# The mask of the single slots, made on ScalarE from the cubic's factor in place of GpSimd

## The chip, the cores and the metric

The kernel runs on one core of a Trainium2 chip. The metric is the device time of one execution in microseconds (us), the median of several runs. The engines are TensorE (PE; its weight loads are PEld), VectorE (DVE), ScalarE (ACT), GpSimd (POOL) and SyncE (SP), which issues most DMAs. Each engine works its own queue in order.

## The reference

A Nystrom attention (batch 4, 8 heads, 576 positions, head dimension 64, 32 landmarks) feeds two MLPs one behind the other, with 2304 tokens, model width 512 and hidden width 2048.

```python
x = attention(q, k, v)                    # A @ Z @ C @ v per head, Z by six Newton steps
h = x @ w_in;  x = (h - tanh(h)) @ w_out  # first MLP
h = x @ w_in2
out = (h * tanh(log(1 + exp(h)))) @ w_out2
```

The change lies in the first MLP, in h - tanh(h). The kernel computes it in two ways and picks one for each element. Where |h| is under 0.28, a cubic form: h times h squared times a factor q, with q = (FB * exp(FK * h^2) + FC)^2. Elsewhere the plain difference h - tanh(h). A mask of one byte per element (0, or not 0) says where the difference is to replace the cubic.

## The kernel before

**Slots.** The first MLP is cut into 128 slots s: batch b = s // 32, half of the positions hf = s // 16 % 2, and one of 16 blocks f = s % 16 of 128 hidden units. A slot works on a tile of 128 hidden units x 288 tokens. Slots 0 to 23 and 104 to 127 are wide: they go in pairs, and an instruction has 576 columns (`vec`). Slots 24 to 103 are single, with 288 columns (`vec_one`). In the trace the single slots run from 112 to 361 us.

**One single slot.** `h1(s)` makes h on TensorE, into one of two PSUM banks of the pool ps_h (L845 to L851; from slot 32 on six matmuls with split operands). `vec_one(s)` then issues, by line of the kernel before:

- ScalarE: e = h squared (L927), t = tanh h (L928), q = exp (L931), q = Square with a bias (L932).
- GpSimd: the mask mk = (e >= FT) (L929), with FT = 0.28^2.
- VectorE: for the slot before, g = q * g (L872, in `small`) and the pick, t over g where the mask is not 0 (L876, in `pick`); for this slot g = h * e (L940) and t = h - t (L942). L942 is the last reader of the bank of h, which `h1(s + 2)` needs.

Two slots later `low_one` splits g into a high and a low part, gg: a copy on ScalarE (L123) and a subtract on GpSimd (L124). Four slots later (LAG) `y1` multiplies gg by the second weight on TensorE, 12 matmuls of 288 columns (L957, L958, L961), into the banks of y. After 16 slots ScalarE empties these banks (L973).

**Beside the slots.** The attention of the next batch and half runs in small steps between the slots, fed in by `bg`: on GpSimd a subtract (L743) and a product (L758) of the softmax, the exp between them on ScalarE (L746), transposes on VectorE (L738, L768), then the split into AT (L123, L124); and the products P of Z and the first weight, which TensorE makes in a bank of ps_m (L431), ScalarE copies (L808) and VectorE splits (L810).

**What sets the order.** For slots 0 to 103 a scheduler orders each engine's instructions by priority; `tc.high_priority(40)` lifts some of them ahead. From slot 104 on the order is as written. In the wide slots the mask is already made by ScalarE, from q (`MASK_BY_ACT` is 0, so in all of them). The constants of that form:

```python
FQ = (FB * exp(FK * FT) + FC) ** 2
FS = 1024.0
V.memset(bias_q, FS * FQ)
A.activation(out=mk, in_=q, func=ACTF.Relu, scale=-FS, bias=bias_q[:, 0:1])
```

q falls as e rises, and FQ is its value at e = FT; so FS * (FQ - q) is above 0 just where e is above FT.

Of the kernel before, what the change touches and what calls it, by code (L numbers as in the profile page):

```python
# [16 lines left out]
ACTF = mybir.ActivationFunctionType  # L17
ALU = mybir.AluOpType
# [5 lines left out]
FT = 0.28 ** 2  # L24
# [5 lines left out]
FS = 1024.0  # L30
# [3 lines left out]
def kernel(  # L34
# [73 lines left out]
    A = nc.scalar  # L108
    G = nc.gpsimd
# [19 lines left out]
    bias_q = const.tile([128, 1], F32)  # L129
# [728 lines left out]
    def low_half(s):  # L858
        gg = gg_tile(s, F32R)
        with tc.high_priority(20):  # L860
            split(sv[s], gg[:, 0], gg[:, 1], late())
        sv[s], sv[s + 1] = gg[:, :, 0], gg[:, :, 1]

    def low_one(s):
        gg = (ggs[s - 1] if s % 2 else gg_tile(s, F32R))[:, :, s % 2]
        with tc.high_priority(20):
            split(sv[s][0], gg[:, 0], gg[:, 1], late())
        sv[s] = gg

    def small(g, q):  # L870
        with tc.high_priority(40):
            V.tensor_tensor(out=g, in0=q, in1=g, op=ALU.mult)  # L872

    def pick(g, mk, t):
        with tc.high_priority(40):
            V.copy_predicated(out=g, mask=mk, data=t)  # L876
# [42 lines left out]
    def vec_one(s):  # L919
        i = s % 2  # L920
        if s == WIDE[0]:
            low_half(s - 2)
        elif s > WIDE[0] + 1:
            low_one(s - 2)
        h, e, q, mk = hp.pop(s), ES[:, i], QS[:, i], MK[-1][:, i]
        t, g = TA[:, i], (TB, TC)[s // 2 % 2][:, i]
        A.activation(out=e, in_=h, func=ACTF.Square)  # L927
        A.activation(out=t, in_=h, func=ACTF.Tanh)  # L928
        G.tensor_scalar(out=mk, in0=e, scalar1=FT, scalar2=None, op0=ALU.is_ge)  # L929
        with tc.high_priority(40):  # L930
            A.activation(out=q, in_=e, func=ACTF.Exp, scale=FK)  # L931
            A.activation(out=q, in_=q, func=ACTF.Square, scale=FB, bias=bias_c[:, 0:1])  # L932
        sv[s] = (g, t, q, mk)
        if s > WIDE[0]:
            g0, t0, q0, mk0 = sv[s - 1]
            small(g0, q0)
            yield 0
            pick(g0, mk0, t0)
            yield 0
        V.tensor_tensor(out=g, in0=h, in1=e, op=ALU.mult)  # L940
        yield 0
        V.tensor_tensor(out=t, in0=h, in1=t, op=ALU.subtract)  # L942
        yield 1
# [424 lines left out]
    def pair(s, bg):  # L1368
        cur[0] = s
        v = vec(s) if wide(s) else None  # L1370
        if s == WIDE[1]:
            two_banks()
        if v:
            h1(s)
            h1(s + 1)
        for i in (s, s + 1):
            cur[0] = i
            if not v:
                h1(i)
            if i >= LAG:  # L1380
                y1(i - LAG, 0)
            mix, tail = bg(i)
            for g in mix + tail:
                part(g)
            if i >= LAG:
                y1(i - LAG, 1)
            parts([v or vec_one(i)] + mix)
            parts(tail)
# [277 lines left out]
```

## Time and profile before

| | us |
|---|---|
| median of 3 runs | 805.53 (805.09 to 805.65) |
| profiled execution | 802.95 |
| its span, first to last instruction | 801.2 |
| PE busy | 776.9 (97%) |
| PEld busy | 694.2 (87%) |
| DVE busy | 639.0 (80%) |
| ACT busy | 576.7 (72%) |
| POOL busy | 202.7 (25%) |

The granted clock of TensorE was 1.00 of full speed over the span. Busy shares are averages over stages with different limits; matmuls are pipelined and their ends are modelled, so a busy PE is not a PE at its peak. In a row of the trace, "[1.27 <-DVE ta L942]" says that the engine had been idle for 1.27 us before the instruction, and that the end of DVE's L942 on tile ta ended that.

### The profile page before, as it was taken

The numbers are of one execution on the slowest core, as the hardware profiler recorded it, in microseconds if no ns is written. First come the engines' busy times: TensorE is split into PE (matmuls) and PEld (weight loads), VectorE is DVE, ScalarE is ACT, GpSimd is POOL, SyncE is SP. The second block draws the span as 40 slices with busy tenths as digits, with TensorE's granted clock in tenths as the row PEclk, the third lists the DMA queues.
The fourth block names the chain that finished last, engine by engine and source line by source line (L and its number), as shares of the span: only waits on it lengthen the run. The fifth ranks groups of instructions, "written<-read, shape, count | busy, mean of one in ns | idle before, by whom it ended". The sixth has DMA issues, their size and how long they took to land.

```text
span 801.2 us, 16889 instructions
## 1 busy us (share of the span) xinstructions
PE 776.9 (97%) x6246; PEld 694.2 (87%) x6247; DVE 639.0 (80%) x1391; ACT 576.7 (72%) x1351; POOL 202.7 (25%) x229
## 2 busy tenths in 40 slices
PE   8889999999999999989999999999999999999997
PEld 4656787899978999778998999998999999999997
DVE  8899899988789976987779988877566876687556
ACT  5788887787678876778999777776556655665553
POOL 0000028765678656772230000001000010001000
PEclk9999999999999999999999999999999999999999
DMA  9788822414035000331215998999998899889881
GB/s 327 299 311 301 333 90 102 148 52 138 13 112 184 6 31 1 106 110 52 83 55 207 388 324 287 357 298 346 367 327 288 283 371 312 288 286 335 293 298 53
DMA packets 79873, 171.47 MB, mean 214 GB/s; under 512 B 8752, under 2 KB 51760, under 8 KB 75696
## 3 DMA queue, kind: packets, MB, share of 16 engines
q1 hardware_dynamic: 78672, 166.73, 60.0%
q0 software_dynamic: 1120, 3.67, 1.2%
q8 instruction: 49, 0.80, 0.4%
q14 instruction: 32, 0.26, 0.1%
HBM read 133.41 MB, written 36.96 MB: 213 GB/s over the span
## 4 chain that ended last, share of the span: by engine, by line
PE 68%; DVE 13%; ACT 10%; issue 4%; POOL 2%; DMA 1%; SPq 0%; DVEq 0%; ACTq 0%; POOLq 0%
PE h L1095 25%; PE y L1095 8%; PE m L1095 4%; PE y L957 3%; PE y L958 2%; PE y L961 2%; PE hw L845 2%; PE y L952 2%; PE y L1228 2%; PE y L1230 2%; PE y L1229 2%; DVE tc L872 2%; DVE tb L872 1%; DVE tb L876 1%; ACT gg L123 1%
## 5 line engine op out<-in xcount | busy, mean ns | idle before, releaser
L1095 PE MATMUL h<-yk,P 128*128 128x256 f32 (+1 forms) x1152 | 182.7, 297 | 0.4 <-DVE yk L1005 0.2
L1095 PEld LDWEIGHTS h<-yk,P 128*128 128x128 f32 x1152 | 161.9, 188 | 6.1 <-DVE u L1170 0.5
L957 PE MATMUL y<-gg,w 128*128 128x288 f32 x448 | 132.8, 311 | 2.9 <-ACT raw L973 2.8
L958 PE MATMUL y<-gg,w 128*128 128x288 f32 x448 | 125.5, 295 | 0.0
L929 POOL TENSOR_SCALAR mk<-es 128x288 uint8<-128x288 f32 x80 | 78.6, 983 | 135.0 <-DVE tc L876 111.5
L957 PEld LDWEIGHTS y<-gg,w 128*128 128x128 f32 x448 | 84.1, 188 | 21.9 <-issue 15.3
L961 PE MATMUL y<-gg,w 128*128 128x288 f32 x448 | 95.5, 294 | 0.0
L958 PEld LDWEIGHTS y<-gg,w 128*128 128x128 f32 x448 | 84.3, 188 | 0.5
L1095 PE MATMUL y<-w,gg 128*128 128x256 f32 x516 | 73.3, 282 | 0.0
L961 PEld LDWEIGHTS y<-gg,w 128*128 128x128 f32 x448 | 71.7, 188 | 0.0
L1095 PEld LDWEIGHTS y<-w,gg 128*128 128x128 f32 x516 | 66.3, 189 | 0.3
L1170 DVE TENSOR_TENSOR w<-w,h 128x256 f32<-128x256 f32 x48 | 20.2, 421 | 56.4 <-PE h L1095 30.9
L124 POOL TENSOR_TENSOR gg<-tc,gg 128x288 fp32r<-128x288 f32 (+1 forms) x45 | 40.0, 898 | 39.7 <-ACT gg L123 35.4
L124 POOL TENSOR_TENSOR gg<-tb,gg 128x288 fp32r<-128x288 f32 (+1 forms) x44 | 40.6, 927 | 32.8 <-ACT gg L123 31.8
L162 ACT ACTIVATE top<-raw 128x512 f16<-128x512 bf16 x56 | 41.9, 783 | 7.8 <-DVE w L167 3.1
L849 PE MATMUL h<-AT,P 128*128 128x288 f32 x144 | 43.0, 299 | 3.0 <-DVE ta L942 3.0
L927 ACT ACTIVATE es<-h 128x288 f32<-128x288 f32 x80 | 32.1, 402 | 17.8 <-PE h L851 15.2
L932 ACT ACTIVATE qs<-qs,bias_c 128x288 f32<-128x288 f32 x80 | 42.7, 534 | 1.2
L1312 POOL DMA_DIRECT2D out_dram<-y x4 | 2.9, 724 | 160.3 <-DVE y L1320 160.3
L850 PE MATMUL h<-AT,P 128*128 128x288 f32 x144 | 42.5, 295 | 0.0
L851 PE MATMUL h<-AT,P 128*128 128x288 f32 x144 | 42.5, 295 | 0.0
L1150 DVE TENSOR_TENSOR gg<-x,gg 128x256 fp32r<-128x256 f32 (+1 forms) x71 | 33.1, 466 | 7.4 <-ACT x L1137 4.5
(265 smaller groups left out, 1995.2 us busy)
## 6 DMA issues: line engine op xcount, KB each, us to landing
P<-w2s SPq DMA_DIRECT2D x24, 1024.0 KB, 5.6
w<-w2t SPq DMA_DIRECT2D x92, 256.0 KB, 8.2
P<-w2s SPq DMA_DIRECT2D x24, 768.0 KB, 7.3
w<-w1s SPq DMA_DIRECT2D x24, 512.0 KB, 4.6
w2s<-P SPq DMA_DIRECT2D x8, 1024.0 KB, 5.8
raw<-in_w2i_dram SPq DMA_DIRECT2D x16, 511.8 KB, 5.0
raw<-in_w2o_dram SPq DMA_DIRECT2D x16, 511.8 KB, 4.3
raw<-in_w1o_dram SPq DMA_DIRECT2D x13, 511.8 KB, 6.2
```

Source lines behind the costliest of these rows:

```text
L124: eng.tensor_tensor(out=L, in0=src, in1=f32(H), op=ALU.subtract)
L162: A.activation(out=top[:, :, 1], in_=raw.bitcast(BF16)[:, :, 2], func=ACTF.Copy)
L849: mm(p, P[:, g, 0, c], AT[:, g, 0, :], start=(g == 0), stop=False)
L850: mm(p, P[:, g, 0, c], AT[:, g, 1, :], start=False, stop=False)
L851: mm(p, P[:, g, 1, c], AT[:, g, 0, :], start=False, stop=(g == NG - 1))
L929: G.tensor_scalar(out=mk, in0=e, scalar1=FT, scalar2=None, op0=ALU.is_ge)
L932: A.activation(out=q, in_=q, func=ACTF.Square, scale=FB, bias=bias_c[:, 0:1])
L957: mm(yps[d], w[:, 0, c], gg[:, 0, :], start=(f == 0), stop=False)
L958: mm(yps[d], w[:, 1, c], gg[:, 0, :], start=False, stop=False)
L961: mm(yps[d], w[:, 0, c], gg[:, 1, :], start=False, stop=(f == NF - 1))
L1095: mm(*args, **kw, skip_group_check=True)
L1150: V.tensor_tensor(out=gg[:, 1, :], in0=x, in1=f32(gg[:, 0, :]), op=ALU.subtract)
```

## The change

In the single slots the mask is made by ScalarE with a Relu on q, behind the Square, and no longer by GpSimd from e. The Relu is written outside the lifted priority. The diff is whole:

```diff
         t, g = TA[:, i], (TB, TC)[s // 2 % 2][:, i]
         A.activation(out=e, in_=h, func=ACTF.Square)
         A.activation(out=t, in_=h, func=ACTF.Tanh)
-        G.tensor_scalar(out=mk, in0=e, scalar1=FT, scalar2=None, op0=ALU.is_ge)
         with tc.high_priority(40):
             A.activation(out=q, in_=e, func=ACTF.Exp, scale=FK)
             A.activation(out=q, in_=q, func=ACTF.Square, scale=FB, bias=bias_c[:, 0:1])
+        A.activation(out=mk, in_=q, func=ACTF.Relu, scale=-FS, bias=bias_q[:, 0:1])
         sv[s] = (g, t, q, mk)
```

Lines 929 to 932 shift by it: exp is L931 before and L930 after, the Square L932 before and L931 after, the new Relu is L932 after. ScalarE has 80 instructions more and GpSimd 80 fewer; the orders of TensorE and of SyncE are the same row for row. VectorE has the same instructions in a slightly different order.

GpSimd in slots 57 to 61, with two subtracts and two products of the softmax (L743, L758). Before:

```order
L743 TENSOR_TENSOR c<-c,xm 128x288
L124 TENSOR_TENSOR gg<-tb,gg 128x288
L929 TENSOR_SCALAR mk<-es 128x288
L743 TENSOR_TENSOR c<-c,xm 128x288
L929 TENSOR_SCALAR mk<-es 128x288
L124 TENSOR_TENSOR gg<-tc,gg 128x288
L758 TENSOR_TENSOR c<-c,xm 128x288
L929 TENSOR_SCALAR mk<-es 128x288
L758 TENSOR_TENSOR c<-c,xm 128x288
L124 TENSOR_TENSOR gg<-tc,gg 128x288
```

And with the change:

```order
L743 TENSOR_TENSOR c<-c,xm 128x288
L124 TENSOR_TENSOR gg<-tb,gg 128x288
L743 TENSOR_TENSOR c<-c,xm 128x288
L758 TENSOR_TENSOR c<-c,xm 128x288
L124 TENSOR_TENSOR gg<-tc,gg 128x288
L758 TENSOR_TENSOR c<-c,xm 128x288
L124 TENSOR_TENSOR gg<-tc,gg 128x288
```

The three masks are gone, and the first L758 stands ahead of a gg subtract that it stood behind.

ScalarE in slot 99, where the last four banks of y of a half are emptied (L973). Before:

```order
L927 ACTIVATE es<-h 128x288
L928 ACTIVATE ta<-h 128x288
L931 ACTIVATE qs<-es 128x288
L973 ACTIVATE raw<-y 128x288
L932 ACTIVATE qs<-qs,bias_c 128x288
L973 ACTIVATE raw<-y 128x288
L808 ACTIVATE P<-m 128x512
L123 ACTIVATE AT<-c 128x288
L808 ACTIVATE P<-m 128x512
L973 ACTIVATE raw<-y 128x288 x2
L123 ACTIVATE gg<-tc 128x288 x2
```

And with the change:

```order
L927 ACTIVATE es<-h 128x288
L928 ACTIVATE ta<-h 128x288
L930 ACTIVATE qs<-es 128x288
L973 ACTIVATE raw<-y 128x288
L931 ACTIVATE qs<-qs,bias_c 128x288
L973 ACTIVATE raw<-y 128x288
L932 ACTIVATE mk<-qs,bias_q 128x288
L808 ACTIVATE P<-m 128x512 x2
L973 ACTIVATE raw<-y 128x288 x2
L123 ACTIVATE gg<-tc 128x288
```

The Relu stands ahead of L808, and the copy into AT, which stood between the two L808, has moved into the next slot.

## Rows read from the trace of the kernel before

**Rows 1.** Busy time by stretch: length; PE, PEld, DVE, ACT, POOL; clock; DMA.

```profile
112.00:139.00 27.00, 25.94 (x205) 20.51 (x203) 24.65 (x53) 20.90 (x53) 20.05 (x22) 1.00 0.17 59
139.00:172.00 33.00, 31.48 (x262) 27.29 (x262) 31.02 (x66) 26.88 (x76) 25.73 (x30) 1.00 0.39 135
172.00:214.00 42.00, 41.95 (x470) 37.98 (x470) 34.10 (x87) 31.95 (x92) 24.92 (x28) 1.00 0.22 72
214.00:240.00 26.00, 24.11 (x209) 20.09 (x209) 22.18 (x51) 18.67 (x50) 18.97 (x22) 1.00 0.25 84
240.00:270.00 30.00, 29.30 (x239) 25.44 (x237) 28.31 (x60) 25.43 (x70) 23.95 (x27) 1.00 0.36 129
270.00:311.00 41.00, 41.00 (x465) 37.63 (x466) 31.30 (x83) 30.89 (x88) 23.82 (x28) 1.00 0.05 16
311.00:339.00 28.00, 26.07 (x225) 22.05 (x224) 24.06 (x56) 19.88 (x53) 20.20 (x24) 1.00 0.22 76
339.00:361.00 22.00, 19.32 (x156) 16.64 (x155) 17.92 (x40) 16.05 (x44) 17.07 (x19) 1.00 0.33 100
```

**Rows 2.** Timeline of PE: start us, us; first h matmul of two neighbouring slots.

```profile
239.22 0.30 PE L849 MATMUL h<-AT,P 128*128 128x288 f32 x1
...
241.61 0.29 PE L849 MATMUL h<-AT,P 128*128 128x288 f32 x1
```

**Rows 3.** Waits, 112 to 360 us: us in total, times, longest us.

```profile
ACT c L746 <- POOL c L743: 7.9, 9, 1.7
...
PEld m L431 <- DVE P L810: 4.5, 6, 1.4
PEld h L849 <- DVE ta L942: 3.9, 4, 1.5
PEld y L957 <- ACT raw L973: 3.7, 4, 2.0
```

**Rows 4.** Groups by line and form, 112 to 360 us: busy us, mean ns | idle before.

```profile
L929 POOL TENSOR_SCALAR mk<-es 128x288 uint8<-128x288 f32 x80 | 78.6, 983 | 135.0 <-DVE tc L876 111.5 <-ACT es L927 18.5
...
L932 ACT ACTIVATE qs<-qs,bias_c 128x288 f32<-128x288 f32 x80 | 42.7, 534 | 1.2
...
L876 DVE COPY_PREDICATED tb<-mk,ta 128x288 f32<-128x288 uint8 x40 | 24.5, 612 | 2.6 <-POOL mk L929 0.5
...
L872 DVE TENSOR_TENSOR tc<-qs,tc 128x288 f32<-128x288 f32 x40 | 23.7, 592 | 1.7 <-ACT qs L932 1.7
...
L940 DVE TENSOR_TENSOR tb<-h,es 128x288 f32<-128x288 f32 x40 | 17.8, 445 | 11.1 <-ACT ta L928 11.1
```

**Rows 5.** Timeline of POOL, ACT and PE, 219 to 231 us, slots 58 to 61.

```profile
219.42 0.93 POOL L929 TENSOR_SCALAR mk<-es 128x288 uint8<-128x288 f32 x1
...
220.43 0.67 POOL L743 TENSOR_TENSOR c<-c,xm 128x288 f32<-128x288 f32 x1
...
221.14 0.45 ACT L746 ACTIVATE c<-c 128x288 f32<-128x288 f32 x1 [1.66 <-POOL c L743]
...
225.23 0.93 POOL L929 TENSOR_SCALAR mk<-es 128x288 uint8<-128x288 f32 x1
...
226.24 0.67 POOL L758 TENSOR_TENSOR c<-c,xm 128x288 f32<-128x288 f32 x1
...
230.97 0.40 PE L849 MATMUL h<-AT,P 128*128 128x288 f32 x1 [1.27 <-DVE ta L942]
```

**Rows 6.** Timeline of POOL and PE, 345 to 349 us, slot 99.

```profile
345.11 1.02 POOL L929 TENSOR_SCALAR mk<-es 128x288 uint8<-128x288 f32 x1
...
346.21 0.67 POOL L758 TENSOR_TENSOR c<-c,xm 128x288 f32<-128x288 f32 x1
...
348.72 0.40 PE L957 MATMUL y<-gg,w 128*128 128x288 f32 x1 [1.77 <-ACT raw L973]
```

**Rows 7.** Timeline of ACT: the Square and the start of its neighbour.

```profile
244.82 0.54 ACT L932 ACTIVATE qs<-qs,bias_c 128x288 f32<-128x288 f32 x1
245.26 0.24 ACT L507 ACTIVATE qb<-red 128x64 f32<-128x64 f32 x1
```

## Prediction, made before the changed kernel was run

> **What bounds the kernel now.** I read three views of the single slots 24 to 103 (112 to 361 us): busy time by stretch, then who waits for whom, then the order of time around the longest waits of TensorE. In the table by stretch the reader should look along the columns [rows 1]. TensorE is busy for 41.95 of 42 us and 41.00 of 41 us in the stretches 172 to 214 and 270 to 311: there it sets the pace, and ScalarE is busy for only 31.95 and 30.89. In the other six stretches TensorE falls short by 0.7 to 2.7 us, and VectorE is the fullest of the others: 31.02 of 33 us and 28.31 of 30 us (94% each) in 139 to 172 and 240 to 270, against 26.88 and 25.43 on ScalarE and 25.73 and 23.95 on GpSimd. Undisturbed, TensorE needs 2.39 us for a slot: its first h matmul starts at 239.22 and that of the next slot at 241.61 [rows 2].
>
> So at most the time that TensorE waits can be won. The waits view names three kinds: its weight loads wait 4.5 us in six places for VectorE's L810 to free a bank of ps_m, 3.9 us in four for VectorE's L942 to free a bank of ps_h, and 3.7 us in four for ScalarE's L973 to empty a bank of y; together 12.1 us. ScalarE in turn waits 7.9 us in nine places for GpSimd's L743 [rows 3].
>
> **What the change removes.** 80 masks at L929 leave GpSimd, 983 ns each, 78.6 us in all [rows 4]. Two things come of it.
>
> First, steps of the attention no longer stand behind a mask. At 219.42 GpSimd makes a mask; only at 220.43 does it start the attention's L743, and ScalarE, whose L746 stands in its queue ahead of the next slot, has been idle for 1.66 us when that is done. At 225.23 the next mask does the same to L758. At 230.97 TensorE has waited 1.27 us for L942, which has come late by both [rows 5]. A mask holds its place on GpSimd for 220.43 - 219.42 = 1.01 us. The new order has no mask between the two L743 and none between the two L758; two masks of 1.01 us cover the 1.27 us, so I take the whole wait as gone. The pattern comes again 97.2 us later, with a wait of like size: 2 x 1.3 = -2.6 us. The same happens in front of the last eviction: a mask at 345.11, L758 behind it at 346.21, and TensorE, at 348.72, has waited 1.77 us for ScalarE's L973 [rows 6]. There the new ScalarE queue also no longer has the AT copy, which waits for that L758, ahead of the last two L973. It has a mask there instead. I take the wait as gone: -1.8 us. In the first stretch two more waits of the kind of rows 3, on L942 and L810, sit behind the same pattern; the stretch falls short by 27.00 - 25.94 = 1.1 us by TensorE's busy time [rows 1], and I count that: -1.1 us. Sum: -2.6 - 1.8 - 1.1 = -5.5 us.
>
> Second, VectorE runs freer. L940, which has one operand in PSUM, takes 445 ns; L872 and L876, which have only SBUF operands of the same size, take 592 and 612 on average [rows 4]. That is 40 x (0.147 + 0.167) = 12.6 us on these two groups; their twins on the other buffer (40 each) bring it to at most twice that, 25 us. In these stretches GpSimd is busy for 174.7 us (its column added up), of which the masks are 78.6, or 45% [rows 1, 4]: I expect 0.45 x 12.6 to 0.45 x 25, 6 to 11 us of VectorE time, to come back. It lies beside TensorE's work and counts only through the waits already taken, so its price is zero; without it the six stretches would not have the room that the next step needs.
>
> The Trainium skill (SBUF — State Buffer, Who interferes with whom) says more: of a VectorE instruction with two SBUF inputs and a GpSimd instruction that reads SBUF, the second to be issued is blocked until the first has finished. By that rule a VectorE instruction behind a mask would lose up to the mask's whole length, where the averages of rows 4 show 0.15 us each; the sum by the rule is the larger gain below.
>
> **What the change adds.** 80 Relus on ScalarE. No row shows them in these slots. The nearest is the Square at L932, with the same 288 columns and also a bias from a tile: 534 ns long [rows 4], but 0.44 us from its start at 244.82 to the next start at 245.26, since neighbours overlap [rows 7]. The bounds are 0.44 and 0.53 us; I take 0.44, because the Relu stands directly behind other work in the new order: 80 x 0.44 = 35.2 us (42.7 at most). The stretches of rows 1 hold 8, 12, 13, 8, 11, 13, 9 and 6 slots, counted by the starts of the Square at L927. In the two stretches that TensorE fills, 13 Relus make 5.7 us against idle time of 10.0 and 10.1 us: hidden. In 214 to 240, 311 to 339 and 339 to 361 they make 3.5, 4.0 and 2.6 us against 7.3, 8.1 and 6.0: hidden, by time that ScalarE now spends waiting for GpSimd. In 139 to 172, 12 Relus make 5.3 us against 6.1; in 240 to 270, 11 make 4.8 against 4.6 [rows 1]. ScalarE would be 97% and over 100% full there, where no engine but TensorE is now above 94%. Packed to that 94%, the work of ScalarE needs 32.2 / 0.94 = 34.2 us and 30.2 / 0.94 = 32.1 us: 1.2 + 2.1 = 3.3 us too long. Of that I charge half, +1.6 us, since ScalarE may fall behind TensorE by two slots (two banks of h, 4.8 us) before TensorE stops, and the stretch that follows has the room to catch up. The ends are 0 and +3.3.
>
> The pick now waits for the Relu instead of GpSimd. The Relu is issued 0.44 us behind the Square and ends about as late as the multiply L872 (0.45 to 0.59 us) that starts on VectorE when the Square ends, and that stands ahead of the pick anyway: zero, up to 0.1 us a slot, and hidden where TensorE leads. Behind the pick on VectorE stands the next slot's L940. Behind the Relu stand, in places, L808 and L973, each 0.44 us later; that is in the 1.6. TensorE's and SyncE's orders are the same to the row, and the wide slots and all that follows are untouched: what is won or lost by 361 us is carried to the end, as the stages behind start from the slots and not from a clock.
>
> **Sum.** -5.5 + 1.6 = -3.9 us. The profiled execution took 802.95 us (span 801.2), 2.6 below the median of the runs, 805.53; its own changed time would be 799.0. I forecast the median: 805.5 - 3.9 = **801.6 us**. About 0.2%, 1.6 us, is what a measurement of this kernel can tell from no change.
>
> **Rivals.**
> - *ScalarE becomes the bound.* If only half of ScalarE's idle time in the six stretches can be filled (half of 6.1 + 6.1 + 7.3 + 4.6 + 8.1 + 6.0 = 38.1 us, so 19.1) while the Relus there need 23.7 us, ScalarE ends 4.6 us later, and L942, L808 and L973 come later with it, so that no wait of TensorE is won: 810.1 us. It decides once less than 62% of that idle time can be filled. For it speaks that much of the idle time lies ahead of instructions that wait in the queue's order; against it, that those waits are for GpSimd and VectorE, which become freer. The Trainium skill (ScalarE: Activation LUTs, Rules for kernel authors) is on this side: it gives relu to VectorE, not to ScalarE. The rows speak against that here, with VectorE at 94% and ScalarE at 81% and 85% where it is tightest.
> - *Nothing is won.* The waits on L810 and L973 stay, since the Relu is now ahead of L808 and L973 on ScalarE as the mask was ahead of L743 and L758 on GpSimd; what is won on L942 pays for the full stretches: 805.5, within 1.6 us.
> - *A larger gain.* All three kinds of waits go, -12.1 us, and nothing is given back: 793.4 us. It needs VectorE to win far more than rows 4 show. The rule of the blocked second instruction (the Trainium skill, SBUF — State Buffer, Who interferes with whom) would bring it about.
>
> That the Relus are not made where the text says is excluded: the order shows 80 on ScalarE and none left on GpSimd.
>
> **How the numbers follow.** The forecast's case (a gain of 1.6 to 8 us) gets 0.50: the places are clear in the trace and come twice, but the gain hangs on a ScalarE that is nearly full. The larger gain gets 0.06, no change 0.21, the slower one 0.23. Faster is 0.56, same 0.21, slower 0.23. The forecast's own range is 797.5 to 803.9; with no change and most of the slower case the range is 797.0 to 809.0, and leaves about 0.15 outside.
>
> **What would show it.** Right: by stretch, ScalarE at 95% or more in 139 to 172 and 240 to 270 and GpSimd about 79 us lower; L872 and L876 near 500 ns; no wait of TensorE on L942 near 231 and 328, none on L973 near 348; the single slots 3 to 5 us shorter, the rest as long as before. Wrong: waits of TensorE for L973, L942 or L810 that are longer than in rows 3, with ScalarE without idle time ahead of them.

## The result and the profile after

The changed kernel takes 798.29 us (median of 4 runs, 797.87 to 799.20), the kernel before 805.31 in the runs beside it (804.38 to 805.65): ratio 0.9914, 95% interval 0.9902 to 0.9926, a gain of 7.0 us where 3.9 were forecast. The profiled execution took 797.99 us, with a span of 796.2, and a granted clock of 1.00 throughout.

Where the time went is first read from the starts of ScalarE's first activation of a slot. From slot 24 to the first wide slot, 104, these rows of the timeline, before:

```profile
112.23 0.41 ACT L927 ACTIVATE es<-h 128x288 f32<-128x288 f32 x1 [1.14 <-PE h L845]
...
360.92 0.65 ACT L889 ACTIVATE es<-hw 128x576 f32<-128x576 f32 x1 [2.22 <-PE hw L851]
```

And after:

```profile
113.07 0.41 ACT L927 ACTIVATE es<-h 128x288 f32<-128x288 f32 x1 [1.14 <-PE h L845]
...
355.64 0.65 ACT L889 ACTIVATE es<-hw 128x576 f32<-128x576 f32 x1 [1.06 <-PE hw L851]
```

The single slots are 248.69 us long before and 242.57 after: 6.1 us shorter. What lies ahead of them and behind them differs by +0.8 and +0.3 us, with the same instructions in it. Counted in the same way from slot 24 on, the changed kernel has won 0.2 us by slot 57, 2.2 by slot 65, 2.4 by slot 89, 4.4 by slot 97 and 6.1 by slot 104. So the gain lies in three places: 2.0 us in slots 57 to 64, 2.0 in 89 to 96, 1.7 in 97 to 103. A second profile of the changed kernel, taken with the last experiments, has 2.0, 2.0 and 1.7 at the same places, but lies 1.4 us behind the first by slot 57: there TensorE waits 1.14 and 0.21 us for VectorE's L686 in slots 51 and 52, which it does not in the first. A reading of a single place can be trusted further than the total of one profile.

Busy time by stretch (columns as in [rows 1]; the borders follow the slots, which now come earlier):

```profile
112.00:139.00 27.00, 26.12 (x219) 20.72 (x212) 23.88 (x54) 22.44 (x58) 11.09 (x13) 1.00 0.15 48
139.00:172.00 33.00, 31.80 (x267) 27.67 (x266) 29.97 (x65) 31.36 (x87) 14.13 (x18) 1.00 0.42 144
172.00:212.00 40.00, 39.37 (x451) 35.62 (x450) 32.65 (x85) 36.51 (x103) 10.09 (x13) 1.00 0.23 76
212.00:237.00 25.00, 24.82 (x218) 20.73 (x216) 20.84 (x49) 23.07 (x61) 11.66 (x16) 1.00 0.23 82
237.00:267.00 30.00, 29.98 (x253) 26.95 (x246) 27.68 (x61) 28.43 (x80) 13.04 (x17) 1.00 0.39 133
267.00:308.00 41.00, 40.37 (x459) 36.30 (x457) 30.51 (x84) 37.34 (x104) 10.89 (x14) 1.00 0.04 16
308.00:334.00 26.00, 25.82 (x225) 22.03 (x224) 22.81 (x54) 23.33 (x61) 11.12 (x15) 1.00 0.23 82
```

ScalarE, the fourth busy time, is at 95% in 139 to 172 and in 237 to 267, as forecast, and in the latter TensorE is full: 29.98 of 30 us. But 172 to 212 and 267 to 308, in which TensorE was full before, now fall short by 0.6 us each. Right behind each of the two full stretches TensorE has a new wait of 0.58 us for VectorE's L537, at 172.74 and at 267.71:

```profile
172.74 1.49 PE L431 MATMUL m<-k,qb 64*32 64x304 f32 x16 [0.58 <-DVE mx L537]
```

Against that, two pairs of short waits around the first evictions are gone: 0.44 us on L973 and 0.22 on L942 at 152.55 and 156.25 before, 0.44 and 0.21 at 249.76 and 253.46. The two sides are about equal, so the gain of the slots does not show them. In 212 to 237 and 308 to 334 TensorE falls short by 0.2 us, where it fell short by 1.9 in the like stretches before [rows 1].

The timeline shows what happened at the first of the three places. GpSimd, the counterpart of [rows 5]:

```profile
218.67 0.67 POOL L743 TENSOR_TENSOR c<-c,xm 128x288 f32<-128x288 f32 x1
...
220.06 0.68 POOL L743 TENSOR_TENSOR c<-c,xm 128x288 f32<-128x288 f32 x1
222.40 0.67 POOL L758 TENSOR_TENSOR c<-c,xm 128x288 f32<-128x288 f32 x1 [1.66 <-DVE xm L756]
...
225.02 0.67 POOL L758 TENSOR_TENSOR c<-c,xm 128x288 f32<-128x288 f32 x1 [0.59 <-DVE xm L756]
```

No mask stands between these rows, and GpSimd waits for its own input, VectorE's xm. ScalarE's L746 comes at 219.37 without a wait and at 220.77 with one of 0.53 us, in place of 1.66. TensorE's timeline before, behind the wait of 1.27 us at 230.97 [rows 5], showed these at the first two places:

```profile
237.08 1.31 PE L431 MATMUL m<-q,kb 64*32 64x288 f32 x16 [0.61 <-DVE P L810]
...
328.18 0.40 PE L849 MATMUL h<-AT,P 128*128 128x288 f32 x1 [1.26 <-DVE ta L942]
334.29 1.31 PE L431 MATMUL m<-q,kb 64*32 64x288 f32 x16 [0.67 <-DVE P L810]
```

After, two waits are left there:

```profile
235.80 1.31 PE L431 MATMUL m<-q,kb 64*32 64x288 f32 x16 [0.18 <-DVE P L810]
...
330.79 1.31 PE L431 MATMUL m<-q,kb 64*32 64x288 f32 x16 [0.17 <-DVE P L810]
```

The wait on L942 is gone at both, and so is most of the wait on L810 that followed 6 us later. In the first stretch nothing of the kind went:

```profile
134.01 1.24 PE L845 MATMUL h<-AT,P 128*128 128x288 f32 x4 [0.88 <-DVE ta L942]
140.74 1.31 PE L431 MATMUL m<-q,kb 64*32 64x288 f32 x16 [1.10 <-DVE P L810]
```

These two were 0.74 and 1.18 us before. The waits of the single slots in all, the counterpart of [rows 3] (112 to 360 us):

```profile
PEld m L431 <- DVE P L810: 3.5, 6, 1.3
ACT c L746 <- POOL c L743: 2.9, 6, 0.8
PEld m L431 <- DVE mx L537: 2.8, 4, 0.8
...
PEld y L957 <- ACT raw L973: 0.9, 3, 0.3
```

The three kinds of waits that were 12.1 us before come to 4.4: the four of L849 on L942 are gone, and the one on L973 ahead of the last eviction is 0.28 us at the weight load and none at the matmul. The wait on L537 was 1.6 us before. Last, the groups that stand beside [rows 4], first two that [rows 4] does not show, before:

```profile
L876 DVE COPY_PREDICATED tc<-mk,ta 128x288 f32<-128x288 uint8 x40 | 24.0, 601 | 2.1
...
L872 DVE TENSOR_TENSOR tb<-qs,tb 128x288 f32<-128x288 f32 x40 | 21.5, 536 | 1.5 <-ACT qs L932 1.0
```

And after:

```profile
L872 DVE TENSOR_TENSOR tb<-qs,tb 128x288 f32<-128x288 f32 x40 | 23.1, 578 | 1.4 <-ACT qs L931 1.3
L872 DVE TENSOR_TENSOR tc<-qs,tc 128x288 f32<-128x288 f32 x40 | 22.6, 566 | 2.1 <-ACT qs L931 1.8
L876 DVE COPY_PREDICATED tb<-mk,ta 128x288 f32<-128x288 uint8 x40 | 22.1, 553 | 2.4
L876 DVE COPY_PREDICATED tc<-mk,ta 128x288 f32<-128x288 uint8 x40 | 20.4, 510 | 3.3 <-ACT mk L932 1.3
...
L932 ACT ACTIVATE mk<-qs,bias_q 128x288 uint8<-128x288 f32 x80 | 42.9, 536 | 1.2
```

The picks fell from 612 and 601 ns to 553 and 510, 6.0 us in all. The multiplies L872 did not get faster: 536 (tb) and 592 (tc) before, 578 and 566 now. Why is taken up in the last section.

### The profile page after: what moved, and what is told of

The parts are those of the page before. It is cut to its first block, busy times and chain, and to the rows that moved or that the text cites. A ratio compares the mean times of both kernels' runs of the same rounds, so it can differ in the third digit from the quotient of the medians.

```text
span 796.2 us, 16879 instructions
## 1 busy us (share of the span) xinstructions
PE 775.6 (97%) x6246; PEld 694.3 (87%) x6247; DVE 632.1 (79%) x1391; ACT 609.0 (76%) x1431; POOL 120.9 (15%) x149
## 4 chain that ended last, share of the span: by engine, by line
PE 68%; ACT 16%; DVE 10%; issue 3%; POOL 1%; DMA 1%; SPq 0%; DVEq 0%; ACTq 0%; POOLq 0%
PE h L1095 25%; PE y L1095 8%; PE m L1095 4%; PE y L957 3%; PE y L961 3%; PE y L958 3%; PE hw L845 2%; PE y L952 2%; ACT qs L931 2%; ACT gg L123 2%; PE y L1228 2%; PE y L1230 2%; PE y L1229 2%; ACT mk L932 1%; ACT qs L930 1%
## 5 line engine op out<-in xcount | busy, mean ns | idle before, releaser
L124 POOL TENSOR_TENSOR gg<-tc,gg 128x288 fp32r<-128x288 f32 (+1 forms) x45 | 39.3, 881 | 192.8 <-PE m L449 114.2
L124 POOL TENSOR_TENSOR gg<-tb,gg 128x288 fp32r<-128x288 f32 (+1 forms) x44 | 39.9, 909 | 79.9 <-ACT gg L123 79.9
L932 ACT ACTIVATE mk<-qs,bias_q 128x288 uint8<-128x288 f32 x80 | 42.9, 536 | 1.2
L931 ACT ACTIVATE qs<-qs,bias_c 128x288 f32<-128x288 f32 x80 | 42.9, 536 | 0.9
L849 PE MATMUL h<-AT,P 128*128 128x288 f32 x144 | 42.6, 296 | 0.0
L1136 ACT ACTIVATE gg<-x 128x256 fp32r<-128x256 f32 (+1 forms) x40 | 18.4, 461 | 26.5 <-DVE x L1170 22.5
```

The source lines that it names most:

```text
L124: eng.tensor_tensor(out=L, in0=src, in1=f32(H), op=ALU.subtract)
L849: mm(p, P[:, g, 0, c], AT[:, g, 0, :], start=(g == 0), stop=False)
```

## The experiments

Three theories are to be told apart. **Q**: the masks stood ahead of the attention's L743 and L758 in GpSimd's queue, and what was late by that stopped TensorE. **V**: each mask slowed VectorE's instructions beside it. **O**: the scheduler's new order on ScalarE won, not the empty GpSimd. And the rival **S**: ScalarE pays for the Relus. Each run is compared with the kernel before on the same chip (805.47, 804.97 and 804.90 us in the three sets):

| run | us | ratio to before | 95% interval |
|---|---|---|---|
| Relu in the 32 attention slots | 798.32 | 0.9906 | 0.9892 to 0.9921 |
| Relu in the 48 others | 806.55 | 1.0012 | 1.0000 to 1.0023 |
| changed, and a spare mask on GpSimd | 803.47 | 0.9974 | 0.9963 to 0.9985 |
| before, L743 and L758 on VectorE | 800.13 | 0.9938 | 0.9924 to 0.9951 |
| Relu in 57 to 62, 89 to 94 | 800.57 | 0.9947 | 0.9933 to 0.9962 |
| Relu in 97 to 100 | 802.82 | 0.9966 | 0.9955 to 0.9978 |
| before, mask on VectorE | 803.19 | 0.9980 | 0.9968 to 0.9993 |
| changed, and a second Relu | 811.83 | 1.0085 | 1.0068 to 1.0102 |
| before, one AT copy behind the eviction | 803.65 | 0.9989 | 0.9980 to 0.9998 |
| Relu in 57 to 62, 89 to 94, 97 to 100 | 798.61 | 0.9919 | 0.9905 to 0.9932 |
| Relu in the 32, L808 and L810 lifted | 796.82 | 0.9903 | 0.9888 to 0.9919 |
| changed, again | 798.10 | 0.9919 | 0.9905 to 0.9932 |

Gains in the text are taken from the ratios, with their intervals. Lines of kernels with added code lie a few higher than in the kernel before.

### Which masks matter: the 32 slots with attention, or the 48 without

```diff
+    ATT = {*range(26, 32), *range(33, 38), *range(57, 63), *range(65, 70), *range(89, 95), *range(97, 101)}
...
+        if not (s in ATT):
+            G.tensor_scalar(out=mk, in0=e, scalar1=FT, scalar2=None, op0=ALU.is_ge)
...
-        A.activation(out=mk, in_=q, func=ACTF.Relu, scale=-FS, bias=bias_q[:, 0:1])
+        if s in ATT:
+            A.activation(out=mk, in_=q, func=ACTF.Relu, scale=-FS, bias=bias_q[:, 0:1])
```

The second kernel has the two conditions the other way round.

> The changed kernel, but the Relu makes the mask only in the 32 single slots in which the attention's steps run (26 to 31, 33 to 37, 57 to 62, 65 to 69, 89 to 94, 97 to 100); in the other 48 GpSimd makes it as before. Theory Q (the masks stood ahead of L743 and L758 in GpSimd's queue): these 32 are all that matters, so the whole gain of 7 us stays, 798 to 799 us. Theory V (each mask on GpSimd slows VectorE's own instructions, in every slot): 32 of 80 of the gain, 7 x 0.4 = 2.8 us, so 802 to 803. Rival S (ScalarE pays for each Relu in the full stretches): 48 Relus less to pay, a little under 798.

> The complement: Relu in the 48 single slots without the attention's steps, GpSimd's mask in the 32 with them. Theory Q: nothing won, 804.5 to 806 us. Theory V: 48 of 80 of the gain, 7 x 0.6 = 4.2 us, so 801. If ScalarE pays for Relus outside the attention's slots, slower than before: above 806.

Measured: 798.32 us, the whole gain, with 32 of the 80 Relus; 806.55 with the other 48, 0 to 1.9 us slower than before. The waits of the first:

```profile
PEld m L432 <- DVE P L811: 3.2, 6, 1.3
...
ACT c L747 <- POOL c L744: 2.3, 5, 0.7
```

And of the second:

```profile
ACT c L747 <- POOL c L744: 9.1, 9, 1.7
...
PEld m L432 <- DVE P L811: 4.5, 6, 1.4
PEld h L850 <- DVE ta L946: 4.0, 4, 1.5
PEld y L961 <- ACT raw L977: 3.6, 4, 2.0
```

The second kernel still has all three kinds of waits of [rows 3], at the same size, with 60% of the masks gone from GpSimd. Theory V, which asked for 4.2 us there, falls; Q, or O within the attention's slots, stands.

### The old masks put back beside the new

```diff
+        if s < 102:
+            G.tensor_scalar(out=spare[:, i], in0=e, scalar1=FT, scalar2=None, op0=ALU.is_ge)
```

> The changed kernel, and GpSimd makes the old mask as well, into a tile that nobody reads (slots 24 to 101): GpSimd's queue and its reads of SBUF are as before, but the pick waits for the Relu. Theories Q and V: the gain goes, 804 to 806 us. Rival P (the pick no longer waits for GpSimd's mask) and rival O (the scheduler's other order on VectorE and ScalarE is what won): the gain stays, 798 to 800.

Measured: 803.47, so 5 of the 7 us go and 2 stay. By slots, nothing is won in 57 to 64 and in 89 to 96 (-0.3 us each), where the changed kernel wins 2.0 each; 0.7 us are lost by slot 57, and 1.4 are won in 97 to 103. Around these places (slots 56 to 65, 88 to 102) ScalarE and VectorE work the same instructions in the same order as in the changed kernel, so at the first two their order alone, theory O, wins nothing. The waits:

```profile
ACT c L746 <- POOL c L743: 5.2, 6, 1.7
PEld m L431 <- DVE P L810: 4.9, 6, 1.5
...
PEld h L850 <- DVE ta L945: 3.4, 2, 1.7
```

L942 and L810 (here L945 and L810) are late again: what GpSimd has in its queue is the cause of most of the gain, and not which engine the pick waits for. But TensorE has no wait on L973 ahead of the last eviction, although the masks are back. There the order of ScalarE is that of the changed kernel, with the AT copy in the next slot. That makes theory O likely for the third place, which a run below takes up.

### The attention's steps taken off GpSimd, the masks left on it

```diff
-        return G if 24 <= cur[0] < NS - 24 else V
+        return V
...
-        split(at, ATt[b, hf][:, g, 0, :], ATt[b, hf][:, g, 1, :], E())
+        split(at, ATt[b, hf][:, g, 0, :], ATt[b, hf][:, g, 1, :], late())
```

> The kernel before, with its masks on GpSimd, but the attention's L743 and L758 are made by VectorE, so that they stand behind no mask; VectorE gets 24 instructions of some 0.45 us more, 11 us. Theory Q: most of the waits of ScalarE on L743 go and the time falls, 799 to 803 us. Theory V: the masks still slow VectorE, which has more to do, so the same or slower, 805 to 810.

Measured: 800.13, 5.0 us (3.9 to 6.1) faster than before with all 80 masks on GpSimd, and with VectorE, the fullest of the three, burdened by 24 instructions of 600 ns:

```profile
L758 DVE TENSOR_TENSOR c<-c,xm 128x288 f32<-128x288 f32 x12 | 7.4, 614 | 0.1
L743 DVE TENSOR_TENSOR c<-c,xm 128x288 f32<-128x288 f32 x12 | 6.8, 584 | 0.0
L746 ACT ACTIVATE c<-c 128x288 f32<-128x288 f32 x12 | 5.3, 443 | 1.5 <-DVE c L743 1.5
```

ScalarE's wait for L743 is 1.5 us in place of 7.9 [rows 3]. This is theory Q from the other side: the two steps had to come out from behind the masks, and either can be moved. The profile, of the slowest of the five runs (801.81 us), bears out the mechanism more than the size: no wait on L942 is left at the two places, but those on L810 behind them are 1.28 and 1.19 us long, and by slots the places win 0.9 and 1.0 us where the changed kernel wins 2.0.

### The places one by one

The edit is that of the first experiment with a shorter set of slots.

> The Relu makes the mask only in slots 57 to 62 and 89 to 94 (12 of 80), the two places where the prediction has the waits on L942; GpSimd elsewhere. Theory Q, by place: the gain that the changed kernel shows there, 2.0 us each, so 4 us and 801 to 802. If it takes masks away over a longer stretch: under 1 us, above 804.5.

> The Relu only in slots 97 to 100 (4 of 80), ahead of the last evictions of y, where the prediction has 1.8 us on L973. Theory Q, by place: 1.7 to 2.4 us, so 803 to 803.8. If that gain came from what was won earlier: none, 805 to 806.

> The Relu in slots 57 to 62, 89 to 94 and 97 to 100 (16 of 80), GpSimd elsewhere. Theory Q with O, by place: 4.4 us from the first two and 2.6 from the last add up to the changed kernel's whole gain, 798 to 799. If Relus elsewhere help or hurt: off that by over 1 us.

Measured: 4.3 us (3.1 to 5.4) by 12 Relus, 2.7 us (1.8 to 3.6) by 4, and 6.5 us (5.5 to 7.6) by the 16 together: the changed kernel, run beside these, wins the same 6.5. By slots the 12 win 2.2 us between slots 57 and 65 and 2.2 between 89 and 97, and nothing elsewhere. The other 64 of the 80 Relus do nothing that these runs can tell.

### The last eviction: order or masks

Here all masks stay on GpSimd, and one copy into AT, the one between the two L808 that the change moves, is issued behind the last two L973.

```diff
-        split(at, ATt[b, hf][:, g, 0, :], ATt[b, hf][:, g, 1, :], E())
+        with tc.issue_after(last_ev[0]) if cur[0] == 101 else ExitStack():
+            split(at, ATt[b, hf][:, g, 0, :], ATt[b, hf][:, g, 1, :], E())
...
-                    A.activation(out=o[:, d], in_=yps[2 * half + d], func=ACTF.Copy)
+                    last_ev[0] = A.activation(out=o[:, d], in_=yps[2 * half + d], func=ACTF.Copy).ins
```

> The kernel before with all its masks on GpSimd; alone the copy into AT that stands between the two L808 ahead of the last two L973 on ScalarE is issued behind those two. TensorE's, VectorE's and SyncE's orders are as before. Theory O (the last eviction's 2 us come from ScalarE's order, in which that copy waits for L768 with L973 behind it): the wait of TensorE on L973 near 348 goes, 2 us less, 803 to 803.8. Theory Q at this place too (the mask at 345.11 makes L758 late, and that is what has to go): no gain, 805 to 806.

Measured: 803.65, a gain of 0.9 us (0.2 to 1.6), between the two expectations. ScalarE's timeline in this run:

```profile
342.22 0.45 ACT L747 ACTIVATE c<-c 128x288 f32<-128x288 f32 x1 [0.72 <-POOL c L744]
...
345.55 0.44 ACT L124 ACTIVATE AT<-c 128x288 fp32r<-128x288 f32 x1 [1.20 <-DVE c L769]
...
348.77 0.75 ACT L975 ACTIVATE raw<-y 128x288 f32<-128x288 f32 x2
```

And TensorE's:

```profile
349.27 0.40 PE L959 MATMUL y<-gg,w 128*128 128x288 f32 x1 [0.48 <-ACT raw L975]
```

The last two evictions no longer wait behind that AT copy, and TensorE's wait falls from 1.77 [rows 6] to 0.48 us. Some of that is paid at the start of the wide slots, where its wait on L942 is 1.48 us in place of 0.80. What is left comes from earlier in ScalarE's queue: 0.72 us for L744 (L743 before) and 1.20 us for the first AT copy, which still stands ahead of the evictions. With Relus in 97 to 100 both AT copies are issued behind the evictions and ScalarE waits for neither. So 0.9 us (0.2 to 1.6) of this place are theory O with all masks left. By slots 97 to 103 this run wins 0.6 us, the run with Relus in 97 to 100 wins 1.7, and the run with the spare masks 1.4: there both copies stand behind the evictions too, although GpSimd makes a mask at 346.31 and starts the second L758 only at 347.42. By these profiles, one of each, most of this place is the order of ScalarE's queue, and a mask ahead of the second L758 costs little once that order is there. To move both copies in the kernel before, without any Relu, was not tried.

### The mask on VectorE

```diff
-        G.tensor_scalar(out=mk, in0=e, scalar1=FT, scalar2=None, op0=ALU.is_ge)
+        V.tensor_scalar(out=mk, in0=e, scalar1=FT, scalar2=None, op0=ALU.is_ge)
```

> The kernel before, its single slots' masks made by VectorE and not by GpSimd, nothing added to ScalarE. Theory Q: the waits of ScalarE on L743 fall as with the change; what is left depends on VectorE's room. 80 masks of some 0.3 to 0.5 us, 24 to 40 us, some 12 to 20 of it in the six stretches where VectorE had about 10 us idle in all: 803 to 812, slower than the changed kernel by 5 us or more. If VectorE has room: 798 to 800.

Measured: 803.19, 1.6 us (0.6 to 2.6) under before and 5 above the changed kernel. The mask itself is cheapest here, 384 ns against 536 on ScalarE and 983 on GpSimd:

```profile
L929 DVE TENSOR_SCALAR mk<-es 128x288 uint8<-128x288 f32 x80 | 30.8, 384 | 8.8 <-ACT es L927 8.3
```

The waits have moved. At the first eviction of y TensorE's wait on L973, 0.44 us before, is now:

```profile
154.10 0.40 PE L957 MATMUL y<-gg,w 128*128 128x288 f32 x1 [1.78 <-ACT raw L973]
```

In the stretch around it, 139 to 172, VectorE is busy for 31.94 of 33 us, 97%. At the start of the wide slots the wait on L942 is 1.92 us, in place of 0.80. The Trainium skill (ScalarE: Activation LUTs, Rules for kernel authors) would give a relu to VectorE. In this kernel the engine with the cheaper instruction was the worse choice. That VectorE had too little room for it is read from its 97%, and not shown by a run of its own.

### How much room ScalarE has left

```diff
+        if s < 102:
+            A.activation(out=spare[:, i], in_=q, func=ACTF.Relu, scale=-FS, bias=bias_q[:, 0:1])
```

> The changed kernel with a second Relu on ScalarE in slots 24 to 101, into a tile that nobody reads: 78 times 0.44 to 0.53 us, 34 to 41 us more for ScalarE, where it has about 21 us idle between 112 and 356. Theory S (ScalarE was at its limit with the first Relu, as the prediction's 1.6 us for full stretches would have it): at least 14 us slower than the changed kernel, 812 or more. If its queue still had much room in the attention's stretches: 799 to 806.

Measured: 811.83, 13.8 us above the changed kernel by the two ratios. Busy time by stretch:

```profile
240.00:270.00 30.00, 28.36 (x228) 24.46 (x227) 27.36 (x58) 29.85 (x83) 13.07 (x16) 1.00 0.49 165
270.00:311.00 41.00, 40.26 (x444) 35.62 (x444) 29.56 (x80) 40.15 (x118) 10.48 (x13) 1.00 0.05 16
```

Now ScalarE is full, 29.85 of 30 and 40.15 of 41 us, and TensorE waits for VectorE's L942 (L945 here), which gets its tanh late:

```profile
PEld h L850 <- DVE ta L945: 8.1, 16, 1.2
```

By the number, the second Relu costs what theory S forecast for it. But that speaks against S for the first one. 78 further Relus of 0.44 us to the next start [rows 7] make 34 us, and the time grew by 14, so 20 us found room beside TensorE's work: there was that much room with the first Relu in. And ScalarE could be filled to 99% in 240 to 270, where the rival had it stop at 62% of its idle time.

### A try at a faster version

```diff
-            A.activation(out=P[:, g, 0, :], in_=p, func=ACTF.Copy)
+            with tc.high_priority(40) if cur[0] >= 24 else ExitStack():
+                A.activation(out=P[:, g, 0, :], in_=p, func=ACTF.Copy)
...
-            V.tensor_tensor(out=P[:, g, 1, :], in0=p, in1=f32(P[:, g, 0, :]), op=ALU.subtract)
+            with tc.high_priority(40) if cur[0] >= 24 else ExitStack():
+                V.tensor_tensor(out=P[:, g, 1, :], in0=p, in1=f32(P[:, g, 0, :]), op=ALU.subtract)
```

> A try at a faster version: the Relu in the attention's 32 slots, and L808 and L810 (copy and split of P) lifted by a priority of 40, since L810 is the largest wait that TensorE still has for an engine, 3.2 us. If L810 came late by what stands ahead of it in the queues: 1 to 3 us under the changed kernel. If it is late by its own inputs: the same, within 1 us.

> The changed kernel itself once more, beside the three others of this set: 798 to 799 us, 0.990 to 0.993 of the kernel before.

Measured: 796.82 us (796.65 to 798.06) against 798.10 (798.03 to 799.22) for the changed kernel in the same set. It is the fastest seen, by 1.3 us, but the two intervals overlap. Its reason was wrong, since the wait it was aimed at is as long as before:

```profile
PEld m L432 <- DVE P L813: 3.1, 6, 1.2
```

By slots it has won 1.2 us by slot 33 and still 1.2 by slot 57, where the changed kernel has won 0.0 and 0.2. The wait of the first stretch on L942 near 134 is gone in it, with a copy into AT and the softmax's small steps in other places of the queues. Which of these moves does it was not tried.

## Why the prediction was right, and where its sizes were off

- **What bounds the kernel**: right. TensorE sets the pace, only its waits could be won, and what the change won (6.1 us of 12.1 in the slots, by the profiles) is waits.
- **The waits on L942, 2 x -1.3**: mechanism right, shown from both sides (masks put back, the attention's steps moved away); the size was too small. Each place gave 2.0 us. The step that failed is that the waits on L810, 6 us behind, were left out of this term. They fell from 0.61 and 0.67 to 0.18 and 0.17 us, since P's split came earlier with the rest of the chain: 1.27 + 0.43 = 1.7 of the 2.0 are in the rows of the first place.
- **The wait on L973, -1.8**: the size was right, 1.7 by slots in the changed kernel and with Relus in 97 to 100 alone (2.7, 1.8 to 3.6, by the times). The prediction named two reasons and did not weigh them: the AT copies' place in ScalarE's queue is most of it (1.4 by slots with the masks put back), and the mask ahead of L758, which it named first, seems the smaller. That the whole wait went is therefore no evidence for the mask.
- **The first stretch, -1.1**: wrong. 0.2 us by slot 57, and the two waits of 0.74 and 1.18 us stand at 0.88 and 1.10. Here TensorE's shortfall was taken as price without a row that ties it to a mask, as [rows 5] does for slot 61; "the same pattern" was assumed.
- **VectorE, 6 to 11 us freer, price zero**: 5.4 us came back (6.0 on the pick, -0.6 on L872), a little under the range, and the price was zero: with 48 masks back on GpSimd the picks took 616 and 547 ns, and the time was the same. The step that failed is that the excess of L872 and L876 was shared out by GpSimd's busy time. Instruction by instruction, the timeline before gives another picture. The 80 multiplies L872 take 9.9 us more than 0.44 us each; 7.4 of these fall on the 25 that start while GpSimd subtracts the low part of gg (L124), which the change leaves there, and 1.8 on the 25 that start while it makes a mask. After, 25 again start behind gg, with 7.6 of 10.6 us. The picks take 10.1 us more than 0.48 each before and 4.1 after; the masks were 1.2 of that, and most of the rest came because 12 picks in place of 22 now start while L124 runs. The size came out near the range for another reason than the one given.
- **The Relus, 0.44 us each**: 536 ns long as the row of the Square said. The charge of +1.6 for full stretches was not paid in sum: between slots 65 and 77 the changed kernel loses 0.2 us, at 95% on ScalarE. The two new waits of 0.58 us on L537 look like such a price, but they stand, with 0.64 us, also in the run with Relus in the attention's slots alone, where ScalarE has no Relu in slots 38 to 56 and 70 to 88; their cause stays open, and the waits that went at the first evictions make up for them. 32 or 16 Relus in place of 80 are not measurably faster either. The lower end of the range, 0, was right.
- **The sum**: -4.0 (two places), -1.7, and -0.2 each by slot 57 and between slots 65 and 89 make the 6.1 us of the profiles, where -5.5 + 1.6 = -3.9 was forecast. So a place too small (-2.6 for 4.0) and a charge that was not paid outweigh a gain that did not come (-1.1). The medians say 7.0 (6.0 to 7.9), while the two profiled executions as wholes differ by 5.0 us (6.1 less 0.8 ahead of the single slots and 0.3 behind): they lie 2.4 and 0.3 under their medians. No view places that difference; the wait on L686 that one profile of the changed kernel has and the other has not is of this kind.
- **The rivals**: ScalarE does become the bound, but one Relu later. "Nothing won" named the Relu ahead of L808 and L973; that order stands in the new queue, and both kinds of waits fell all the same. The larger gain needed VectorE to win much more. The Trainium skill's rule for it (SBUF — State Buffer, Who interferes with whom) lets a blocked VectorE instruction wait for the whole of GpSimd's. Behind L124 the trace agrees: a multiply that starts 0.1 us behind such a subtract of 0.80 us is 1.02 us long (230.84, last section). Behind a mask it does not: of the 25 multiplies that start while a mask runs, 8 lose over 0.05 us, and none over 0.26, though a mask is 0.98 us long on average. The prediction set the 0.15 us of rows 4 against the rule; that is an average over multiplies that were blocked and others that were not, and could not test it. Most of the blocking comes from L124, which stays.

## What to carry to other kernels

An engine that is busy for a quarter of the time can still set the pace by what stands in front of what in its queue: look for the short step with many waiters behind a long one that nobody hurries for. Sixteen of eighty instructions, at three places, held the whole gain here, and the places could be named beforehand from the timeline around TensorE's longest waits; a stretch's shortfall without such a row was not worth its price. And a wait that is removed takes the next one along, so follow the chain past the first wait before giving it a size.

## What was not expected of the hardware

The multiply L872, with two SBUF operands, takes 436 ns on average when no GpSimd instruction is running as it starts (27 of 80 in the kernel before; the longest 459). One that starts while GpSimd subtracts gg is held until that is done: 22 of 25 end 0.31 to 0.32 us after the subtract, whether they started early in it or late. One of them in full, and one that started behind the mask at 219.42 [rows 5]:

```profile
230.75 0.80 POOL L124 TENSOR_TENSOR gg<-tb,gg 128x288 fp32r<-128x288 f32 x1
230.84 1.02 DVE L872 TENSOR_TENSOR tb<-qs,tb 128x288 f32<-128x288 f32 x1
...
219.50 0.65 DVE L872 TENSOR_TENSOR tc<-qs,tc 128x288 f32<-128x288 f32 x1
```

Behind a mask it is held more briefly: this one ends 0.19 us before the mask does, and so do all 8 that lose anything to speak of. L940, with one operand in PSUM, is never over 458 ns, although 72 of 80 start while GpSimd works. So the average of such a group says how often it met the other engine's subtract, not how busy that engine was: L872 stayed at 536 and 592 ns, then 578 and 566, with GpSimd's work down from 174.7 to 93.0 us. The same mask, 128x288 to one byte, took 384 ns on VectorE, 536 on ScalarE and 983 on GpSimd.
